# Eighteen routing pieces called four attention positions earlier in an attention-then-experts kernel

## The chip, the core and the metric

The kernel runs on one core of a Trainium2 chip. The metric is the device time of one launch in microseconds; the time before is the median of three runs. The engines are named as in the profile: PE (matmul), PEld (its weight load), DVE (vector), ACT (scalar), POOL (GpSimd) and SP, which here only issues transfers.

## What is computed

Chunked attention over 8 sequences of 576 tokens with 8 heads of 64, whose output x (4608 tokens of 512 numbers) goes through a mixture of 8 experts. Which expert a token uses depends on its own logits and, through a gate, on the token before it.

```
scores = scale * q_chunk @ k_chunk.T            # chunks of 64 tokens
attn   = softmax(scores);  x = attn @ v_chunk   # x: [B, S, 512]
logits = x @ w_gate;  gate = sigmoid(x @ w_local)
for b, s:                                       # in order along a sequence
    e = argmax(logits[b, s]) if s == 0 or gate[b, s] < 0.5 else prev_e
    h = relu(x[b, s] @ w1[e])                   # 512 -> 1024
    out[b, s] = p[e] * (h @ w2[e])              # 1024 -> 512
```

## The kernel before, in words

**Attention.** The 4608 tokens are cut into 18 attention tiles of 256 (numbers 0 to 17). A software pipeline runs iterations i = 1 to 15 (loop at L845). In each, PE does, in the order of the string `steady`: scores of tile i+1 (L214), transposes of the finished x of tile i-2 (L177, `tx`), the first half of the value products of tile i-1 (L263, `va`), transposes of q and k of tile i+2 (L177, `tq`), the router's logits of tile i-2 (L306), the second half of the values, two small logit transposes (L317, L319) and the transposes of the softmax numbers of tile i (`tp`). DVE takes the maxima (L225), subtracts them (L228), divides the value products (L275 to L277) and writes the logits to `L` (L326). The second half of the values reuses the PSUM tile `o` that DVE's first division reads, so PE waits for that division. POOL copies q and k of tile i+3 into pairs of heads (L169, token `pr`), which PE transposes in the next iteration.

**Transfers.** SP issues every load of q, k, v and weights, and the stores of finished x tiles to the DRAM buffer `x_d` (L335), in one fixed order. A load of v into one of three buffers waits until PE has done with that buffer. The finished tiles of the first iterations stand in spare weight space; tiles 6 to 8 and 14 to 17 share three buffers named `xs`, so the division of tile 17 cannot write until the store of tile 14 has read its buffer out.

**Routing of the first half.** When the logits of tokens 0 to 2303 (18 blocks of 128, attention tiles 0 to 8) are known, eighteen pieces sort them by expert: the fresh choice (s1a, s1b), the gate's scan along the sequence (s2 to s8), one-hots and counts (s9 to s11), the rank within an expert (`rank`), `after_a`, one-hot rows `rh` by rank (L452, of which twelve go to POOL and six to DVE), and two steps that turn them by 18 small matmuls (L587) into the index lists `gidx` and `sidx`. The last piece, `early_gather`, has POOL gather the first two blocks of 128 sorted tokens from `x_d` into raw1[0] and raw1[1] (L626). The pieces are called at "hooks" in the steady loop: position 4i + h is hook h of iteration i (h0 after DVE's maxima, h1 and h2 after the two router steps, h3 at the end). A list of numbers sets them.

**Around it.** Weights w1 of expert 0 land in raw1 and are split into a rounded part (ACT, L841) and a remainder (POOL, L842) at the end of iteration 13 (parts 0 and 1) and 15 (part 2). The store of x tile 8 is also called at the end of iteration 13. After iteration 15 comes the drain, a hand-written order in which the last attention tiles, the second half's routing and the first three expert blocks of 128 tokens are mixed; `x0` in it transposes gathered block 0 (L620). Then one expert block follows another (L659, L673) to the end.

Of the kernel before, what the change touches and what calls it, by code (L numbers as in the profile page):

```python
# [59 lines left out]
    "t2": "AVAA",  # L60
    "steady": "lq s*8 s h0 tx*8 s va*4 va tq*8 ra*2 h1 tq*8 pr*4 va*4 lv va ra*2 h2 tp*8 s h3 ",
    "stores": {5: (0,), 6: (1,), 7: (2,), 8: (3,), 9: (4,), 10: (5,), 11: (6,), 12: (7,), 13: (8,), 14: (9,), 15: (10, 11)},
    "hooks": [47, 47, 49, 49, 51, 51, 53, 54, 55, 55, 57, 58, 58, 59, 59, 61, 62, 62],
}


# [1076 lines left out]
```

## Time and profile before

| | us |
|---|---|
| median of 3 runs | 667.67 (667.2 to 672.87) |
| the profiled execution | 668.65 |
| its span in the profile | 666.8 |
| PE busy | 629.7 (94%) |
| DVE busy | 361.2 (54%) |
| ACT busy | 264.9 (40%) |
| POOL busy | 149.8 (22%) |

The span goes from the first to the last instruction; 1.85 us of the profiled execution lie around it. Busy shares are means over stages with different limits; in timelines a bracket gives the idle time before a row and what ended it.

### The profile page before, as it was taken

The page shows a single profiled execution, that of the slowest core. Times are in us where ns is not written, and L with a number is a line of the kernel's source. Part 1 is how long each engine was busy: PE and PEld are TensorE (multiplying, and loading weights), DVE is VectorE, ACT ScalarE, POOL GpSimd, SP SyncE. Part 2 cuts the span into 40 slices and gives each one's busy share as a digit, 9 for nine tenths or more (in the row PEclk, how much of TensorE's full clock was granted, in tenths as well). Part 3 has the DMA queues.
Part 4 walks back from the last instruction along what each step waited for, and adds up shares of the span by engine and source line. Part 5 has one row for each costly group of instructions (what it writes and reads, how often), then busy time and mean ns, then how long its engine had stood idle before and what let it go on. Part 6 is the DMA issues. An engine that isn't in the chain of part 4 may idle for free.

```text
span 666.8 us, 16364 instructions
## 1 busy us (share of the span) xinstructions
PE 629.7 (94%) x5684; PEld 501.7 (75%) x5684; DVE 361.2 (54%) x936; ACT 264.9 (40%) x439; POOL 149.8 (22%) x214
## 2 busy tenths in 40 slices
PE   3899999988999999999999999999999999999993
PEld 2778788765678877778888777788877888768882
DVE  1667768784895566662422566642566423564230
ACT  2667676755412244451221453512455222442220
POOL 3422333562040212121211212121121211112101
PEclk9999999989999999999999999999999999999998
DMA  8999999999723114644111154550248511244101
GB/s 199 261 207 271 255 257 251 275 234 322 228 80 102 62 39 163 198 170 148 50 50 34 47 179 166 172 184 33 78 146 281 182 34 35 66 160 169 48 19 38
DMA packets 85420, 98.22 MB, mean 147 GB/s; under 512 B 42388, under 2 KB 61844, under 8 KB 85268
## 3 DMA queue, kind: packets, MB, share of 16 engines
q1 hardware_dynamic: 71236, 61.01, 32.7%
q0 software_dynamic: 6640, 20.65, 9.5%
q10 hardware_dynamic: 7392, 14.68, 6.5%
q8 instruction: 77, 1.26, 0.8%
q14 instruction: 75, 0.61, 0.3%
HBM read 77.28 MB, written 20.35 MB: 146 GB/s over the span
## 4 chain that ended last, share of the span: by engine, by line
PE 44%; issue 27%; DMA 22%; DVE 4%; SPq 1%; POOLq 1%; POOL 1%; DVEq 0%
DMA out<-ysb,sidx 14%; PE y L673 12%; PE h L659 12%; PE tr L177 7%; DMA qk<-in_k 4%; PE o L263 3%; PE sc L214 2%; PE tr L753 2%; DMA x_d<-xs 1%; PE lg L306 1%; SPq L140 1%; DMA raw<-x_d,gidx 1%; PE tr L738 1%; PE y L680 1%; PE h L667 1%
## 5 line engine op out<-in xcount | busy, mean ns | idle before, releaser
L673 PE MATMUL y<-w2h,hp 128*128 128x512 f32 x560 | 185.8, 401 | 1.2 <-ACTq L1021 1.2
L659 PE MATMUL h<-w1h,xp 128*128 128x512 f32 x560 | 161.5, 398 | 0.0
L788 POOL DMA_INDIRECT out<-ysb,sidx x41 | 40.8, 995 | 371.4 <-DVE ysb L785 284.1
L673 PEld LDWEIGHTS y<-w2h,hp 128*128 128x128 f32 x560 | 105.2, 188 | 24.9 <-ACTq L978 1.4
L659 PEld LDWEIGHTS h<-w1h,xp 128*128 128x128 f32 x560 | 102.1, 188 | 20.0
L673 PE MATMUL y<-w2l,hp 128*128 128x512 f32 x280 | 110.6, 395 | 0.0
L659 PE MATMUL h<-w1l,xp 128*128 128x512 f32 x280 | 87.3, 393 | 0.5 <-DVEq L978 0.5
L726 ACT CAST hp<-tr 128x512 fp32r<-128x512 f32 x64 | 34.9, 589 | 119.9 <-PE tr L753 117.2
L785 DVE TENSOR_SCALAR ysb<-y,ppr 128x512 f32<-128x512 f32 x35 | 26.2, 750 | 87.4 <-PE y L673 72.3
L659 PEld LDWEIGHTS h<-w1l,xp 128*128 128x128 f32 x280 | 52.5, 188 | 12.4 <-DVEq L978 1.0
L673 PEld LDWEIGHTS y<-w2l,hp 128*128 128x128 f32 x280 | 52.7, 188 | 11.1 <-DVEq L978 0.2
L712 ACT ACTIVATE hsb<-h 128x1024 f32<-128x1024 f32 x35 | 35.9, 1026 | 59.4 <-PE h L659 56.5
L169 POOL COPY qk<-qk 128x512 f32<-128x512 f32 x69 | 40.4, 617 | 80.9 <-PE tr L177 53.4
L727 DVE TENSOR_TENSOR xp<-tr,xp 128x512 fp32r<-128x512 f32 x32 | 22.1, 690 | 59.8 <-ACTq L978 57.1
L177 PE MATMUL tr<-ident,qk 128*128 128x128 f32 x288 | 42.5, 293 | 12.0 <-POOL qk L169 5.5
L727 DVE TENSOR_TENSOR hp<-tr,hp 128x512 fp32r<-128x512 f32 x64 | 41.6, 685 | 15.8 <-ACT hp L726 14.1
L645 ACT ACTIVATE pex<-pex 128x8 f32<-128x8 f32 x41 | 8.6, 210 | 102.6 <-DVE pex L644 90.7
L167 ACT COPY qkT<-tr 128x512 f32<-128x512 f32 x69 | 37.6, 589 | 28.3 <-PE tr L177 21.0
L177 PEld LDWEIGHTS tr<-ident,qk 128*128 128x128 f32 x288 | 33.3, 149 | 19.5 <-POOL qk L169 9.3
L626 POOL DMA_INDIRECT xg<-x_d,gidx x39 | 41.2, 1056 | 14.1 <-issue 10.1
L753 PEld LDWEIGHTS tr<-ident,hsb 128*128 128x128 f32 x274 | 32.0, 140 | 9.0 <-ACTq L978 3.3
L753 PE MATMUL tr<-ident,hsb 128*128 128x128 f32 x274 | 37.3, 274 | 1.4 <-DVEq L978 1.4
(213 smaller groups left out, 798.8 us busy)
## 6 DMA issues: line engine op xcount, KB each, us to landing
raw<-in_moe_w SPq DMA_DIRECT2D x14, 1024.0 KB
raw<-in_moe_w ACTq DMA_DIRECT2D x14, 1024.0 KB, 7.6
raw<-in_moe_w SPq DMA_DIRECT2D x16, 512.0 KB, 4.2
qk<-in_q SPq DMA_DIRECT2D x11, 512.0 KB, 7.0
qk<-in_k SPq DMA_DIRECT2D x11, 512.0 KB, 8.3
v<-in_v SPq DMA_DIRECT2D x22, 256.0 KB, 5.5
x_d<-xs SPq DMA_DIRECT2D x7, 521.0 KB, 8.1
x_d<-x_w2h SPq DMA_DIRECT2D x6, 521.0 KB, 6.6
```

The lines of the kernel that those rows point to most:

```text
L167: eng.copy(dst, src)
L169: eng.tensor_copy(dst, src)
L177: nc.tensor.transpose(box["ps"][:, n], src_of(n), ident)
L626: nc.gpsimd.indirect_dma_start(out=dst, out_offset=None, in_=src, in_offset=bass.IndirectOffsetOnAxis(ap=gidx[t].bitcast(U32), axis=0))
L659: nc.tensor.matmul(hs[:, j], xs[a][:, c], W1[w][c][:, 512 * j:512 * j + 512], start=(c == 0 and n == 0), stop=(c == 3 and n == 2))
L673: nc.tensor.matmul(y, hx[f // 4][a][:, f % 4], W2[w][c][:, f % 2, :], start=(f == 0 and n == 0), stop=(f == 7 and n == 2))
L712: nc.scalar.activation(hsb, hs.rearrange("p j f -> p (j f)"), AF.Relu)
L726: nc.scalar.copy(p[:, 0], ps)
L727: V.tensor_tensor(p[:, 1], ps, p[:, 0].bitcast(F32), ALU.subtract)
L753: nc.tensor.transpose(ps[:, n], hsb[:, at + P * n:at + P * n + P], ident)
L785: either(kind and kind[1], lambda: V.tensor_scalar(ysb, y, pr, None, ALU.mult), lambda: y_part(ysb, y, pr))
L788: nc.gpsimd.indirect_dma_start(out=out, out_offset=bass.IndirectOffsetOnAxis(ap=sidx[t].bitcast(U32), axis=0), in_=ysb, in_offset=None, bo ...
```

## The change

One list of numbers differs. Every one of its eighteen entries is smaller by 4, so each routing piece is called exactly one iteration earlier, at the same hook in it. No instruction is added or removed. SP's order is the same row for row.

```
-    "hooks": [47, 47, 49, 49, 51, 51, 53, 54, 55, 55, 57, 58, 58, 59, 59, 61, 62, 62],
+    "hooks": [43, 43, 45, 45, 47, 47, 49, 50, 51, 51, 53, 54, 54, 55, 55, 57, 58, 58],
```

On POOL, around the end of iteration 13, before: `qk_2486` to `qk_2489` are the pair copies for attention tile 16, `qk_2665` to `qk_2668` those for tile 17, `w1l` the remainders of the weights, and the rows named DMA the gathers.

```order
L169 COPY qk_2489<-qk 128x512
L842 TENSOR_TENSOR w1l_77<-raw_0_83,w1h_73 128x512 x2
L842 TENSOR_TENSOR w1l_78<-raw_0_83,w1h_74 128x512 x2
L169 COPY qk_2665<-qk 128x512
L169 COPY qk_2666<-qk 128x512
L169 COPY qk_2667<-qk 128x512
L169 COPY qk_2668<-qk 128x512
L452 TENSOR_SCALAR rh<-iota_m,rq 128x128 x12
L626 DMA raw_0_83<-x_d,gidx_2921 128x521 x2
```

The same place on POOL in the changed kernel, where the copies for tile 17 are named `qk_2708` to `qk_2711`:

```order
L169 COPY qk_2499<-qk 128x512
L452 TENSOR_SCALAR rh<-iota_m,rq 128x128 x12
L842 TENSOR_TENSOR w1l_77<-raw_0_83,w1h_73 128x512 x2
L842 TENSOR_TENSOR w1l_78<-raw_0_83,w1h_74 128x512 x2
L169 COPY qk_2708<-qk 128x512
L169 COPY qk_2709<-qk 128x512
L169 COPY qk_2710<-qk 128x512
L169 COPY qk_2711<-qk 128x512
L626 DMA raw_0_83<-x_d,gidx_2768 128x521 x2
```

The twelve one-hot rows moved from behind four weight remainders and four pair copies to ahead of them; the two gathers still follow the copies.

On DVE, behind the rank pieces (their last rows are L834 and the six L452), a piece of the difference: which tile's maxima (L225) and subtractions (L228) stand there, those of scores called in iteration 15 (`mx_2790`) before and those of iteration 14 (`mx_2630`) now.

```order
 L834 TENSOR_SCALAR cnt<-cnt 128x1
 L452 TENSOR_SCALAR rh<-iota_m,rq 128x128 x6
-L225 TENSOR_REDUCE mx_2790<-sc 128x8
-L225 TENSOR_REDUCE mx_2792<-sc 128x8
-L228 TENSOR_TENSOR pr<-sc,mx_2790 128x512
-L228 TENSOR_TENSOR pr<-sc,mx_2792 128x512
+L225 TENSOR_REDUCE mx_2630<-sc 128x8
+L225 TENSOR_REDUCE mx_2632<-sc 128x8
+L228 TENSOR_TENSOR pr<-sc,mx_2630 128x512
+L228 TENSOR_TENSOR pr<-sc,mx_2632 128x512
```

The same batch of rank work moved ahead of the softmax of the iteration before.

## Rows read from the trace of the kernel before

**Rows 1.** The page's head and its first part: busy us, share, instructions.

```profile
span 666.8 us, 16364 instructions
PE 629.7 (94%) x5684; PEld 501.7 (75%) x5684; DVE 361.2 (54%) x936; ACT 264.9 (40%) x439; POOL 149.8 (22%) x214
DMA  8999999999723114644111154550248511244101
```

**Rows 2.** PE's waits over the whole run: us in total, times, longest.

```profile
PE o L263 <- DVE xs L277: 2.7, 2, 2.4
PE tr L620 <- DMA raw<-x_d,gidx: 2.6, 1, 2.6
```

**Rows 3.** Windows: length, busy us of PE, PEld, DVE, ACT, POOL; clock, DMA, GB/s.

```profile
86.64:94.08 7.44, 7.44 (x173) 6.16 (x172) 5.42 (x15) 5.25 (x10) 2.34 (x4) 1.00 0.94 254
...
125.33:133.35 8.02, 7.85 (x175) 6.42 (x174) 5.73 (x15) 6.37 (x12) 6.57 (x7) 1.00 1.09 263
133.35:145.35 12.00, 9.53 (x191) 7.73 (x190) 11.35 (x48) 5.51 (x10) 7.68 (x14) 0.86 0.92 232
```

**Rows 4.** Timeline of DVE in iteration 15: start, us, instruction.

```profile
133.39 0.45 DVE L427 TENSOR_TENSOR_SCAN inc<-tr,zrow 128x144 f32<-128x144 f32 x1
...
137.63 1.27 DVE L225 TENSOR_REDUCE mx<-sc 128x8 f32<-128x512 f32 x2
...
140.44 0.69 DVE L277 TENSOR_TENSOR xs<-o,rs 128x512 f32<-128x512 f32 x1
```

**Rows 5.** Timeline of PE, iteration 15 to the start of the drain.

```profile
133.35 1.16 PE L214 MATMUL sc<-qkT 64*64 64x64 f32 x64
...
136.10 1.09 PE L177 MATMUL tr<-ident,qk 128*128 128x128 f32 x8
...
141.19 0.70 PE L263 MATMUL o<-v,pT 64*64 64x65 f32 x32 [2.41 <-DVE xs L277]
...
145.35 1.16 PE L214 MATMUL sc<-qkT 64*64 64x64 f32 x64
```

**Rows 6.** Timeline of POOL, iterations 14 and 15.

```profile
126.78 4.99 POOL L842 TENSOR_TENSOR w1l<-raw,w1h 128x512 fp32r<-128x512 f32 x4 [3.44 <-ACT w1h L841]
131.69 2.30 POOL L169 COPY qk<-qk 128x512 f32<-128x512 f32 x4
136.33 7.04 POOL L452 TENSOR_SCALAR rh<-iota_m,rq 128x128 bf16<-128x128 bf16 x12 [2.34 <-DVE qsA L832]
146.18 1.18 POOL L626 DMA_INDIRECT raw<-x_d,gidx  x1 [2.81 <-issue]
```

**Rows 7.** Timeline of PE in the drain, its two longest waits there.

```profile
154.03 0.63 PE L620 MATMUL tr<-ident,raw 128*128 128x128 f32 x4 [2.65 <-DMA raw<-x_d,gidx]
...
167.80 0.35 PE L263 MATMUL o<-v,pT 64*64 64x65 f32 x8 [1.10 <-DVE xs L326]
```

**Rows 8.** Timeline of DVE in the drain, the division of tile 17.

```profile
166.96 0.69 DVE L277 TENSOR_TENSOR xs<-o,rs 128x512 f32<-128x512 f32 x1 [1.77 <-DMA x_d<-xs]
```

**Rows 9.** The chain that ended last: start, us, two transfers of it.

```profile
146.18 7.71 DMA raw<-x_d,gidx
...
158.21 8.65 DMA x_d<-xs
```

**Rows 10.** Timeline of SP, the last load of v and the store of tile 14.

```profile
141.92 1.45 SPq L153 DMA_DIRECT2D v<-in_v  x2
...
158.21 0.37 SPq L335 DMA_DIRECT2D x_d<-xs  x1
```

**Rows 11.** Windows of 2 us in the drain, columns as in rows 3.

```profile
142.00:144.00 2.00, 1.93 (x25) 1.68 (x25) 1.90 (x9) 0.00 (x0) 1.37 (x3) 0.50 0.70 250
...
152.00:154.00 2.00, 0.00 (x0) 0.00 (x1) 0.32 (x1) 0.00 (x0) 0.39 (x1) 1.00 1.03 273
...
162.00:164.00 2.00, 2.00 (x33) 1.49 (x31) 1.61 (x2) 0.00 (x0) 0.00 (x0) 1.00 1.05 392
164.00:166.00 2.00, 2.00 (x31) 1.61 (x22) 0.37 (x2) 1.17 (x2) 0.00 (x0) 1.00 0.71 171
```

## The prediction

> **What bounds the kernel now.** I read the page's first two parts first: PE is busy 94% of 666.8 us, so only time in which PE stands still is to be won, and the line of DMA digits shows the transfers near full through the first 180 us [rows 1]. Then PE's waits over the whole run: two of those in the stretch that the change touches are long, 2.4 us for a DVE division and 2.6 us for a gather [rows 2]. The windows by iteration show where the first lies: a steady iteration takes 7.44 us, the last one 12.00, with PE busy for 9.53 of it [rows 3]. The timelines of DVE, PE, POOL and SP from 125 to 168 us show the rest.
>
> In the last steady iteration, which starts at 133.35, DVE works off the rank pieces of the routing from 133.39 until the maxima get their turn at 137.63: 4.24 us in front of the softmax. The division that PE's second half of the values waits for is pushed to 140.44, and PE stands for 2.41 us until 141.19 [rows 4, 5]. That is the first wait. In the drain PE stands for 2.65 us until 154.03, because gathered block 0 is issued at 146.18 and lands 7.71 us later [rows 6, 7, 9]. At 167.80 PE waits again, for 1.10 us: the row names DVE's L326, but in front of that DVE itself idled 1.77 us for the store of an x tile, and its division, the work PE needs, ends at 167.65 [rows 7, 8]. That store is tile 14's: issued at 158.21, landed 8.65 us later [rows 9, 10].
>
> **The change, part by part.** The instructions are the same; eighteen pieces run one iteration earlier. So the sum has moved waits in it and nothing else.
>
> 1. *The wait for the division moves and stays.* The rank batch now stands ahead of the softmax of the iteration that began at 125.33 [rows 3]. I take its new start as 125.5, since two small matmuls of the routing now come ahead of it. The batch is 4.24 us long there too and finds the same work behind it, so that iteration takes about 12.0 us instead of 8.02 and ends near 137.5; the last one loses the batch. Effect: 0. Bounds: nothing saved, or the part that came from the clock. In the window from 142 to 144 the granted clock was 0.50, its lower level of 1.2 GHz, after PE's 2.41 us of standing, and the whole iteration had 0.86 [rows 3, 11]; that is up to 12.00 x 0.14 = 1.7 us. Whether the clock falls again after the moved wait is open; the 2.65 us wait at 152 to 154 left it at 1.00 [rows 7, 11]. By point 2 it makes no difference which it is.
>
> 2. *POOL gets a queue.* The twelve one-hot rows took 7.04 us and began 136.33 - 133.35 = 2.98 us after the start of their iteration [rows 5, 6]. Before, only the gathers were behind them. Now four weight remainders (4.99 us) and the four pair copies for tile 17 (2.30 us) are. Rows from 125.5 + 3.0 = 128.5 to 135.5, remainders to 140.5, copies to 142.8, instead of 131.69 to 133.99. PE asks for the first copy 136.10 - 133.35 = 2.75 us into its iteration, near 140.3, and gets it at 140.5 + 0.6 = 141.1: a new wait of 0.8 us. Had the iteration before been shorter by the clock's share, PE would only wait longer here. From there a steady iteration has 7.44 - 2.75 = 4.7 us left [rows 3, 5], so the drain starts near 145.8 instead of 145.35. Effect: +0.4 us. The remainders themselves are not needed before the drain's first expert block.
>
> 3. *The gather goes out earlier.* Its list is ready well before POOL is free, so it is issued behind the copies, near 142.9 instead of 146.18, and with the same 7.71 us lands near 150.6. PE asks for it 154.03 - 2.65 = 151.4, plus 0.4: 151.8. The 2.65 us wait goes. Effect so far: +0.4 - 2.65 = -2.2 us.
>
> 4. *What is late next.* This is the step that decides. 2.2 us earlier, PE comes to the division of tile 17 at 166.70 - 2.2 = 164.5. That division waits for the store of tile 14 to land [rows 8, 9]. Its issue follows PE, so it goes out near 156.0 instead of 158.2. But the windows show the transfer engines full all the way, 1.03 from 152 to 154 and 1.05 from 162 to 164, with the share falling to 0.71 only from 164 on, just before the store's landing at 166.86 [rows 9, 11]. A transfer that waits behind a full queue lands when the queue has been worked off, not 8.65 us after its issue. The queue holds the same loads and stores; so the landing stays at about 166.9, and PE's wait there grows from 1.1 to about 3.3 us. Bounds of the effect: +2.2 (landing fixed) or 0 (landing moves with the issue); I take +2.2, nearest to the rows on DMA share. On this the Trainium skill says, in "DMA: Bandwidth & Descriptors", section "Queues, rings and completion order", that a transfer engine consumes a ring's descriptors in ring order and takes turns between queues by packets. By that the store, on SP's queue, waits for all older loads; the share of 1.05 agrees, and the sum by the rule is the one here, 0 net, while the issue's 8.65 us taken as a latency would give -2.2.
>
> 5. *SP's queue could also come late.* The last load of v is issued at 141.92, right when PE's second half of the values, which ends at 141.19 + 0.70 = 141.89, lets the buffer go [rows 5, 10]. Without the wait that half would have started 141.19 - 2.41 - 136.10 = 2.7 us after the first transposes; now these start at 141.1, so it runs from 143.8 to 144.5, and SP's later stores and loads stand behind the load for 2.6 us more. Bounds: 0, if enough older transfers are still queued, or the whole 2.6 us on the landing of point 4. The two earlier gathers use the room in the meantime (the share was 0.70 from 142 to 144 [rows 11]) and no longer lie between the loads at 150 to 154. I take +0.2.
>
> Sum: 0 + 0.4 - 2.65 + 2.25 + 0.2 = +0.2 us. The span would be 667.0 instead of 666.8, the execution 668.85 instead of 668.65. That execution lies 0.98 above the median of the runs; against the median, 667.67 + 0.2 = 667.9. After 168 us nothing is moved.
>
> **The rivals.**
>
> *The gain comes through (faster).* The landing of tile 14's store moves with its issue, and point 4 costs nothing. For it: the share of 0.71 at 164 to 166 shows a queue that is nearly empty when the store lands, so an earlier issue could profit a little. Against it: everything before 164. Time: 667.67 + 0.4 - 2.65 = 665.4.
>
> *SP falls behind (slower).* The one mechanism is the last load of v, held back by PE's wait on POOL's late copies. If the transfer engines run dry at 144 to 146, all 2.6 us reach the landing at 166.9, and PE with it: 667.67 + 2.6 = 670.3. It decides from the point at which the queue in front of that load is shorter than 2.6 us. For it: at 142 to 144 the share is already down to 0.70. Against it: the gathers fill that gap.
>
> *The clock pays.* The wait of point 4 is then PE's longest in the drain, 3.3 us. If the clock falls behind it as it fell behind 2.41 us, that costs up to 1.7 us: 669.6. The Trainium skill, "TensorE: Matmul & The Clock Gate", section "What's actually happening", says that the default state is throttled and activity releases it, which speaks for such a loss behind any long wait. Here one wait of about 2.5 us shows it and one does not [rows 11].
>
> *Nothing moves.* If POOL's queue is longer than counted and the gather goes out no earlier than 146, the old waits stay: 667.7. Within the likeliest case's range.
>
> **How the numbers follow.** The wait moves and the time stays: 0.55, with its own range from 667.2 to 668.8. Gain comes through: 0.2. SP falls behind: 0.12. The clock pays: 0.13. The forecast is 667.9. The range of 8 in 10 reaches to the rivals on both sides, from 665.2 to 670.6. About 1% (6.7 us) is what a measurement of this kernel can tell from no change. No case gets there by itself, the two slow ones together not either; what is left is for something I have not seen: faster 0.02, same 0.95, slower 0.03.
>
> **What would show it.** Right: in the changed profile the 2.4 us wait for the division stands near 131 to 133; POOL's copies for tile 17 start near 140.5 and PE waits about a microsecond for them; the gather is issued near 143 and the 2.65 us wait on it is gone; the wait at the division of tile 17 is 3 us or more and ends within half a microsecond of 167.8. Wrong in point 4: that wait stays near 1 us and ends near 165.6. Wrong in point 2: PE does not wait for the copies, or waits more than 3 us. Wrong in point 5: the store of tile 14 lands after 168. Wrong altogether: a difference that is already there before 125 us or arises after 200.

## The result, and the profile after

The change makes the kernel a little slower: 675.16 us (672.04 to 680.43) against 671.88 (667.2 to 677.02) for the kernel before on the same chip, a ratio of 1.0057 with the 95% interval [1.0035, 1.0080]. The forecast was 667.9 against 667.67, a ratio of 1.0003, and its range ended at 670.6, a ratio of 1.0044. Against the 671.88 of this chip the loss is 3.3 us by the medians, 3.8 by the ratio.

The profiled execution of the changed kernel took 675.16 us, its median. That of the kernel before took 668.65, which lies 3.2 us below the median of its later runs, so of the 6.5 us between the two profiles (spans of 673.3 and 666.8) about half is that draw, that is, chance in which execution was profiled. Head of the page after, to be laid beside [rows 1]:

```profile
span 673.3 us, 16364 instructions
PE 632.6 (94%) x5684; PEld 503.7 (75%) x5684; DVE 367.8 (55%) x936; ACT 265.0 (39%) x439; POOL 150.7 (22%) x214
```

The same instructions, but DVE is busy for 6.6 us more. That should not happen when work is only moved. Windows over three stretches, up to the start of iteration 11, from there to the division of tile 17, and the rest (length, busy us of PE, PEld, DVE, ACT, POOL; clock, DMA, GB/s). Before:

```profile
0.00:101.50 101.50, 86.97 (x1884) 71.85 (x1884) 61.23 (x149) 60.94 (x105) 34.31 (x89) 1.00 0.99 240
101.50:168.00 66.50, 58.61 (x1205) 46.72 (x1204) 48.38 (x150) 41.27 (x72) 29.61 (x39) 0.97 1.00 275
168.00:666.80 498.80, 484.13 (x2604) 383.11 (x2597) 251.60 (x638) 162.73 (x263) 85.86 (x86) 0.99 0.33 111
```

After:

```profile
0.00:101.00 101.00, 87.29 (x1884) 72.24 (x1884) 61.41 (x149) 60.93 (x105) 34.35 (x89) 1.00 0.98 240
101.00:174.00 73.00, 61.21 (x1206) 48.47 (x1205) 54.74 (x150) 41.31 (x72) 29.44 (x39) 0.95 0.92 253
174.00:673.00 499.00, 484.12 (x2596) 382.98 (x2595) 251.66 (x638) 162.73 (x263) 86.94 (x86) 1.00 0.33 111
```

The 6.5 us arise in the middle stretch alone, and so do DVE's 6.4. The transfer engines' share fell from 1.00 to 0.92. The timeline of DVE after, at the place where the index lists are made:

```profile
138.72 0.15 DVE L590 COPY inv<-tr 128x6 f32<-128x6 f32 x1
138.91 6.49 DVE L592 SCALAR_TENSOR_TENSOR id<-inv 128x3 f32<-128x3 f32 x1
145.32 0.16 DVE L595 CAST gidx<-inv 128x3 int32<-128x3 f32 x1
...
149.47 0.69 DVE L277 TENSOR_TENSOR xs<-o,rs 128x512 f32<-128x512 f32 x1
```

An instruction on 128x3 numbers lasts 6.49 us; in the profile before it took 0.16:

```profile
144.05 0.16 DVE L592 SCALAR_TENSOR_TENSOR id<-inv 128x3 f32<-128x3 f32 x1
```

The timeline of POOL after, beside [rows 6]:

```profile
131.20 7.04 POOL L452 TENSOR_SCALAR rh<-iota_m,rq 128x128 bf16<-128x128 bf16 x12 [4.58 <-DVE qsA L832]
138.21 4.95 POOL L842 TENSOR_TENSOR w1l<-raw,w1h 128x512 fp32r<-128x512 f32 x4
143.11 2.27 POOL L169 COPY qk<-qk 128x512 f32<-128x512 f32 x4
147.37 1.18 POOL L626 DMA_INDIRECT raw<-x_d,gidx  x1 [1.99 <-issue]
```

The long instruction ends at 145.40, and POOL's four remainders and four copies end at 145.38. Before, POOL stood idle when the index lists were made (144.05 to 145.5, [rows 6]). The softmax (from 146.65) and the division of iteration 15 stand behind that instruction on DVE. PE after, beside [rows 5, 7]:

```profile
125.32 0.55 PE L177 MATMUL tr<-ident,qk 128*128 128x128 f32 x3 [1.69 <-issue]
...
143.77 1.21 PE L177 MATMUL tr<-ident,qk 128*128 128x128 f32 x8 [1.63 <-POOL qk L169]
...
150.22 1.15 PE L263 MATMUL o<-v,pT 64*64 64x65 f32 x32 [3.65 <-DVE xs L277]
...
159.56 0.60 PE L620 MATMUL tr<-ident,raw 128*128 128x128 f32 x4
...
173.53 0.35 PE L263 MATMUL o<-v,pT 64*64 64x65 f32 x8 [1.32 <-DVE xs L326]
```

PE waits 1.63 us for the pair copies and then 3.65 us for the division. The wait of 2.65 us for the gathered block at L620 is gone. At 125.32 a standstill of 1.69 us ends, for which the profile names no cause (`issue`); the kernel before did not have it at that place. The windows of iterations 13 to 15, beside [rows 3]:

```profile
118.45:129.48 11.03, 9.34 (x175) 7.65 (x174) 6.82 (x21) 4.78 (x8) 2.40 (x4) 0.85 1.09 291
129.48:139.33 9.85, 8.56 (x191) 6.63 (x191) 9.44 (x35) 6.96 (x13) 8.13 (x13) 1.00 0.92 246
139.33:153.70 14.37, 9.10 (x173) 7.49 (x173) 12.56 (x23) 5.35 (x10) 8.18 (x10) 0.88 0.56 150
```

PE began iteration 13 of the kernel before here:

```profile
116.95 1.16 PE L214 MATMUL sc<-qkT 64*64 64x64 f32 x64
```

So the changed kernel is 1.5 us late at the start of iteration 13, 4.15 at that of iteration 14 (129.48 against 125.33) and 5.98 at that of iteration 15 (139.33 against 133.35). In this pair of profiles most of the lag is there before the long instruction begins at 138.91; iteration 15 adds 2.4 us to it, and the drain gives 2.8 back by block 0. What the long instruction costs can therefore not be read from this pair; it takes a kernel that differs in nothing else (`psum_all` below).

In iteration 15 the transfers run at a share of 0.56, where they had 0.92 before. SP's waits show one reason: it held the next loads of v back until PE let a buffer go (waits in total, how many, the longest).

```profile
SPq L153 <- PE o L263: 15.1, 2, 11.6
```

So the reading is that a small DVE instruction beside POOL's queue stops DVE, DVE stops PE, and PE stops SP's queue. The experiments test the first link, and what it costs.

### The profile page after: what moved, and what is told of

It is laid out like the page before. It is cut to its first block, busy times and chain, and to the rows that moved or that the text cites. A ratio compares the mean times of both kernels' runs of the same rounds, so it can differ in the third digit from the quotient of the medians.

```text
span 673.3 us, 16364 instructions
## 1 busy us (share of the span) xinstructions
PE 632.6 (94%) x5684; PEld 503.7 (75%) x5684; DVE 367.8 (55%) x936; ACT 265.0 (39%) x439; POOL 150.7 (22%) x214
## 4 chain that ended last, share of the span: by engine, by line
PE 45%; issue 26%; DMA 20%; DVE 5%; SPq 1%; ACT 1%; POOLq 1%; POOL 0%; DVEq 0%
DMA out<-ysb,sidx 14%; PE y L673 12%; PE h L659 12%; PE tr L177 7%; DMA qk<-in_k 3%; PE o L263 3%; PE sc L214 2%; PE tr L753 2%; DMA x_d<-xs 1%; SPq L140 1%; PE lg L306 1%; PE tr L738 1%; PE y L680 1%; DVE id L592 1%; PE lg L317 1%
```

## The experiments

Ratios are to the kernel before on the same chip. In the expectations, theory P is that DVE is shut out while POOL works on SBUF. Theory C stands for chance in `again`, and for code that arrives late from `light_queue` on.

**again: the change once more.** No edit.

> The changed kernel once more, unedited. Its first profile had four things that the prediction did not: DVE's L592, 3 numbers wide, took 6.49 us beside POOL's remainders and pair copies (it took 0.16 us before); PE waited 3.65 us for the division behind it; PE stood 1.69 us in the middle of transposes for nothing that the profile names; and the clock fell twice. Theory P (DVE is shut out while POOL works on SBUF): L592 is again over 5 us and ends with POOL's last pair copy, and the division costs PE 3 us or more again. Theory C (a chance of that one execution): L592 is near 0.2 us here. Both expect the 1.69 us standstill to be gone or elsewhere, and a ratio to the kernel before of 1.003 to 1.008.

Measured: 675.05 us, ratio 1.0049 [1.0015, 1.0083]. L592 lasts 6.49 us again, from 140.33 on, beside POOL's remainders and copies, which end at 146.80. PE's standstill between the transposes returns with 2.43 us. So neither the loss nor the long instruction nor the standstill is a chance of one execution.

**psum_operand: the two-operand instructions read one operand from PSUM.** `pv` is the product in PSUM, of which `inv` is the copy in SBUF; L598 and L602 likewise. Their result `id1` is kept in PSUM, so L599 and L604 read that there.

```
-            V.scalar_tensor_tensor(id1, inv[:, 0], float(P), inv[:, 1], ALU.mult, ALU.add)
+            V.scalar_tensor_tensor(id1, pv[:, 0], float(P), inv[:, 1], ALU.mult, ALU.add)
```

> The changed kernel, but in the last routing step of the first half every DVE instruction that took two operands from SBUF takes one of them from PSUM (id1 is kept in PSUM, the others read the matmul's result there). Same work, same order, POOL untouched. Theory P with two operands (POOL shuts out only DVE instructions that read two tensors from SBUF): the step's ten instructions take about 0.2 us each, 2 us together, PE's wait for the division in the last iteration falls from 3.65 to under 1 us, and the time falls by 2.5 to 5 us against the changed kernel, to a ratio near 0.997 to 1.000. Rival, any DVE instruction that reads SBUF is shut out: the next one that reads only SBUF (the integer ones on gidx) takes 5 to 6 us instead, and the ratio stays at 1.005. Rival, the late pair copies alone make the loss: the ratio stays at 1.005 with L592 short.

Measured: 671.82 us, ratio 1.0023 [0.9989, 1.0057]. DVE at that place:

```profile
136.93 0.17 DVE L593 SCALAR_TENSOR_TENSOR tr<-tr,inv 128x3 f32<-128x3 f32 x1
137.00 6.34 DVE L596 CAST gidx<-inv 128x3 int32<-128x3 f32 x1
```

The instruction with a PSUM operand takes 0.17 us, and the next one, a cast from SBUF to SBUF with one source, is held for 6.34 instead. So it is not only a matter of two SBUF sources. On the price this run decides nothing: its interval holds both no loss and that of the change.

**one_input: POOL's four remainders of parts 0 and 1 become plain copies.** The subtraction is left out, so the first expert's numbers are not the reference's.

```
+                nc.gpsimd.tensor_copy(lo, raw) if c < 2 else
                 nc.gpsimd.tensor_tensor(lo, raw, hi.bitcast(F32), ALU.subtract)
```

> The changed kernel, but POOL's four remainders of parts 0 and 1 of w1 are plain copies of the raw weights, which read one tensor instead of two (the subtraction of the rounded part is left out). Theory P with POOL's two-operand instructions as the cause: L592 falls to about 0.2 us. Theory P with any POOL instruction that reads SBUF: L592 still lasts until POOL's last pair copy, about 4 x 0.6 + 2.3 = 4.7 us after the copies begin, less what of them had run before L592. Copies are shorter than subtractions (0.6 instead of 1.24 us), so PE's wait for the pair copies (1.63 us) goes in either case, and the time falls by 1 to 4 us against the changed kernel.

Measured: 671.98 us, ratio 1.0002 [0.9963, 1.0040]; L592 is held 3.81 us, from 140.91 until the end of POOL's copies at 144.71. A POOL run with one source per instruction holds DVE too; it is only shorter.

**splits_late: the remainders behind the pair copies, the gather at 60.**

```
-        for c in {13: (0, 1), 15: (2,)}.get(i, ()):
+        for c in {14: (0, 1), 15: (2,)}.get(i, ()):
```

> The changed kernel, but the split of parts 0 and 1 of w1 (ACT's rounding, POOL's remainder) is called at the end of iteration 14 instead of 13, and the gathers two hooks later, behind it. All work kept. POOL then has only the pair copies behind the one-hot rows. Theory P: beside the last routing step POOL runs the pair copies alone; if copies shut DVE out too, L592 takes about 2.3 us, if only the remainders do, 0.2 us; PE waits under 0.5 us for the copies; ratio 0.994 to 1.000, since the gather comes out about as late as before and its wait in the drain partly returns. Rival, the loss comes from the rank batch in front of iteration 14's softmax: the ratio stays at 1.005.

Measured: 672.74 us, ratio 1.0014 [0.9979, 1.0049]; L592 is held 1.56 us, until the four copies end. In all four runs the hold ends with POOL's uninterrupted run, whatever its length. Their times, though, can't be told from one another: a shorter hold is not shown to be a shorter kernel.

**kinds and kinds_mid: which DVE instructions are held, beside which POOL work.** Two kernels of their own. They leave the computation out. In the first each small instruction starts at the same moment as POOL's run, in the second it comes 0.7 us into it, and POOL's instructions write to different tiles.

> A kernel of its own that leaves the whole computation out and writes one tile to the output: nine kinds of small DVE instruction (128x3) are each released by a memset of POOL that is followed at once by a run of POOL work on other tiles: 4 subtractions of 128x512, 8 copies of 128x512, 8 one-hot rows of 128x128 bf16, 12 memsets of 128x512. Theory P1 (any DVE instruction with a source and a destination in SBUF and no PSUM operand is shut out until POOL's run ends): scalar_tensor_tensor, tensor_tensor, tensor_scalar, copy, cast last 4 to 5 us beside the subtractions, about 4 us beside the copies. Theory P2 (only two SBUF sources, and casts and copies): tensor_scalar, reciprocal and the reduction stay under 0.3 us. Both: sources in PSUM are not held, and nothing is held beside memsets, which read nothing; beside the bf16 one-hot rows the traces showed no held instruction, so under 0.7 us.

> The kernel of small DVE kinds again (it leaves the whole computation out), with two differences: POOL's instructions write to different tiles, so that none waits for the one before it, and DVE first reduces 128x512 (about 0.6 us, never held), so that the small instruction arrives while POOL's first or second instruction is running. POOL runs: 4 subtractions; 8 copies; 8 bf16 one-hot rows; 2 subtractions then 4 copies. Theory R (DVE must wait until POOL's queue of SBUF work has run dry): scalar_tensor_tensor, tensor_tensor, tensor_scalar, copy and cast last 3.5 to 4.5 us beside the subtractions and 3 to 4 us beside the copies. Theory I (it waits for the running instruction only): at most 1.3 and 0.6 us. Both: reciprocal, reduction and instructions with PSUM stay under 0.3 us, and nothing is held beside the bf16 rows.

Timeline of DVE in `kinds`, two rows beside POOL's memsets:

```profile
156.31 0.16 DVE L52 TENSOR_TENSOR tt<-tok 128x3 f32<-128x3 f32 x1 [6.74 <-POOL tok L65]
163.29 0.53 DVE L53 TENSOR_SCALAR ts<-tok 128x3 f32<-128x3 f32 x1 [6.82 <-POOL tok L65]
```

Timeline of DVE in `kinds_mid`: beside subtractions, three beside copies, one with an operand in PSUM, and one beside subtractions followed by copies:

```profile
3.10 0.62 DVE L53 SCALAR_TENSOR_TENSOR stt<-tok 128x3 f32<-128x3 f32 x1
...
47.49 3.75 DVE L53 SCALAR_TENSOR_TENSOR stt<-tok 128x3 f32<-128x3 f32 x1
...
52.16 0.41 DVE L54 TENSOR_TENSOR tt<-tok 128x3 f32<-128x3 f32 x1
...
70.31 0.17 DVE L58 RECIPROCAL rec<-tok 128x3 f32<-128x3 f32 x1
...
83.76 0.15 DVE L61 SCALAR_TENSOR_TENSOR stp<-tok,ps 128x3 f32<-128x3 f32 x1
...
149.08 3.98 DVE L57 CAST casti<-tok 128x3 int32<-128x3 f32 x1
```

Held beside fp32 subtractions and copies in `kinds_mid`: scalar_tensor_tensor, tensor_tensor, tensor_scalar, copy and cast, where all operands lie in SBUF. In `kinds` the same five were not held beside the subtractions, with whose run they start (0.16 to 0.17), and beside the copies for one copy only (0.61 to 0.62), where theory P1 had 4 to 5 us and about 4. Never held in either (0.15 to 0.18): reciprocal, reduction, and whatever has a PSUM operand. Beside the bf16 one-hot rows they took at most 0.32 us. For how long varies: in `kinds_mid` ten of the fifteen instructions of these five kinds beside fp32 work came through at the next change of POOL's instruction (0.41 to 0.62 us), two at a later change (2.87, 3.43), three only at the end of the run (3.75 to 3.98). Neither theory R nor I holds alone: at each change of POOL's instruction DVE may get in or not. In the seven profiles of attention kernels with a hold it never got in before the end of the run.

The Trainium skill, "SBUF — State Buffer", sections "SBUF: two separate sides" and "Who interferes with whom", says that DVE and GpSimd share a pair of ports as an exclusive lock, taken by copies, casts and tensor_scalar in their two-port forms, and by instructions with two SBUF inputs against a GpSimd instruction that reads SBUF, and that reductions never contend. The kinds of the two runs agree as far as the page names them, also that memsets held the tensor_scalar (0.53) and not the tensor_tensor (0.16). It says further that the loser waits for the instruction that came first. Here it waited for up to eight; the measurement stands.

**held_before: the hold put into the kernel before.** POOL's halves of the first two splits move behind the one-hot rows, which is at the end of iteration 14; ACT's halves stay.

```
-            run(w1_split(c))
+            run(w1_split(c)[0::1 + (c < 2)])
...
-    hq = sg + [lambda: run(sg_rank()), after_a, lambda: run(sg_onehots())] + sl + [early_gather]
+    hq = sg + [lambda: run(sg_rank()), after_a, lambda: (run(sg_onehots()), [run(w1_split(c)[1::2]) for c in (0, 1)])] + sl + [early_gather]
```

> The kernel before with POOL's four remainders w1l of parts 0 and 1 called behind the one-hot rows of iteration 15 instead of at the end of iteration 13 (ACT's halves stay). POOL then subtracts from about 143.4 to 148.4, just when DVE makes the index lists (144.05). Theory P: L592 or a neighbour of it, 0.16 us before, lasts 3.5 to 5 us and ends with POOL's last remainder; the gather is issued near 149.5 to 151 instead of 146.18, and the kernel is slower than before by 2 to 4 us (ratio 1.003 to 1.006). Theory N (long rows on DVE beside POOL are a peculiarity of the moved order): L592 stays at 0.16 us, the gather is near 148.5, behind the remainders in POOL's order, and the kernel is slower by at most 2.4 us (ratio up to 1.0035).

Measured: 679.78 us, ratio 1.0110 [1.0069, 1.0151]. DVE:

```profile
144.30 4.28 DVE L592 SCALAR_TENSOR_TENSOR id<-inv 128x3 f32<-128x3 f32 x1
```

POOL:

```profile
143.59 4.96 POOL L842 TENSOR_TENSOR w1l<-raw,w1h 128x512 fp32r<-128x512 f32 x4
150.55 1.18 POOL L626 DMA_INDIRECT raw<-x_d,gidx  x1 [2.00 <-issue]
```

PE:

```profile
158.81 1.09 PE L620 MATMUL tr<-ident,raw 128*128 128x128 f32 x4 [4.96 <-DMA raw<-x_d,gidx]
```

The hold appears in the old order as soon as POOL is at work there, and ends with POOL's last remainder at 148.55. The loss, some 7 us, is larger than the 2 to 4 us expected, and not all of it is the hold: the gather is 4.4 us later than in [rows 6], of which POOL's new order alone was expected to make 2.3 (148.5). The profile is of one of the two shortest of its six runs. In it PE waits 4.96 us for the gather instead of 2.65, and behind that wait the granted clock was 0.50, its lower level of 1.2 GHz, which the kernel before did not show there.

**psum_all: the change without the hold.** Every one of the small instructions of the first list gets an operand in PSUM (`pv`, `gp`, `od`, `pad`), by keeping scratch numbers beside the product.

```
+                gp, od, pad = pinv[:, 260:260 + Q].bitcast(I32), pinv[:, 280:280 + Q], pinv[:, 300:300 + Q]
...
-            V.tensor_copy(gi, inv[:, 0])
+            V.tensor_copy(gp, pv[:, 0])
...
-            V.scalar_tensor_tensor(odd, odd, float(HT), id1, ALU.mult, ALU.add)
+            V.scalar_tensor_tensor(od, od, float(HT), id1, ALU.mult, ALU.add)
```

> The change, with every small DVE instruction of the index lists (L592 to L604 there) given one operand in PSUM, by keeping the scratch numbers beside the product in the same PSUM bank; same instructions, same order, same results. Theory P (DVE is shut out only where all its operands are in SBUF, while POOL has SBUF work): none of the ten lasts over 0.5 us, PE's wait for xs L277 after the pair transposes of iteration 15 (3.65) falls under 1 us, and the time falls by 2 to 4 us against the change: ratio to before 0.998 to 1.002. Theory Q (the hold is a detour that costs nothing; the loss comes from the early pieces, POOL's later pair copies and the late block of code): the long instruction is gone, but the ratio stays at 1.003 to 1.007.

Measured: 670.54 us, ratio 0.9997 [0.9963, 1.0031]. DVE:

```profile
136.76 0.16 DVE L599 SCALAR_TENSOR_TENSOR id<-tr,inv 128x3 f32<-128x3 f32 x1
136.83 0.16 DVE L600 CAST tr<-tr 128x3 int32<-128x3 f32 x1
```

POOL:

```profile
136.05 4.96 POOL L847 TENSOR_TENSOR w1l<-raw,w1h 128x512 fp32r<-128x512 f32 x4
140.95 2.28 POOL L169 COPY qk<-qk 128x512 f32<-128x512 f32 x4
143.41 1.18 POOL L631 DMA_INDIRECT raw<-x_d,gidx  x1 [0.17 <-POOL qk L169]
```

PE, and the chain that ended last:

```profile
133.90 0.70 PE L263 MATMUL o<-v,pT 64*64 64x65 f32 x32 [1.25 <-DVE x_w2l L277]
...
168.19 0.35 PE L263 MATMUL o<-v,pT 64*64 64x65 f32 x8 [2.32 <-DVE xs L326]
```

```profile
157.39 9.87 DMA x_d<-xs
```

With POOL's order unchanged and only the operands' place changed, the hold is gone and with it the loss: 1.0057 - 0.9997 = 0.0060, some 4 us of 671, though the two intervals leave 1 to 7. This is the run that decides for P. In its profile iteration 15 takes 8.70 us (137.74 to 146.44) where the change takes 14.37, at about the same granted clock (0.87 and 0.88). A standstill of 1.69 us is in this profile too, so it is not what `psum_all` wins.

**s2_late, pair_first, choice_early: the change in parts.** `s2_late` keeps the last two pieces at 62. `pair_first` keeps fourteen pieces early and restores POOL's order. `choice_early` moves the first twelve alone.

```
-    "hooks": [43, 43, 45, 45, 47, 47, 49, 50, 51, 51, 53, 54, 54, 55, 55, 57, 58, 58],
+    "hooks": [43, 43, 45, 45, 47, 47, 49, 50, 51, 51, 53, 54, 54, 55, 55, 57, 62, 62],
+    "hooks": [43, 43, 45, 45, 47, 47, 49, 50, 51, 51, 53, 54, 54, 55, 58, 59, 62, 62],
+    "hooks": [43, 43, 45, 45, 47, 47, 49, 50, 51, 51, 53, 54, 58, 59, 59, 61, 62, 62],
```

> The change with its last two pieces (the turn of the one-hots into index lists, and the gather) left at position 62, the other sixteen at 43 to 57. POOL's copies and remainders then end before the index lists are made. Theory P (the loss is DVE shut out by POOL's run of SBUF work): L592 lasts under 0.3 us instead of 6.49; PE's wait for xs L277 after the pair transposes of iteration 15 (3.65) falls under 1 us; the ratio to before is 0.998 to 1.003, with the gather near 148 to 150 and some of the wait of 2 to 2.65 for it back. Theory Q (the loss comes from the early fourteen pieces themselves: the pieces' work on DVE and the standstill of 1.3 to 2.4 us in PE's transposes after L422): L592 may be short, but the ratio stays at 1.004 to 1.007.

> The first fourteen pieces as in the change (positions 43 to 55, the rank at 54), but the one-hot rows at 58, behind the pair copies of iteration 14, then 59, 62, 62: POOL's order is that of the kernel before row for row. No hold, no wait for POOL's pair copies. Theory Q1 (loss by POOL's order and the hold): the division wait of 2.4 us is gone, PE's standstill at the code block (1.3 to 2.4) stays, the wait for gathered x is 1 to 2.7: ratio 0.997 to 1.001. Theory Q2 (loss by the pieces' earlier work on DVE and PE itself): ratio 1.003 to 1.007 with POOL's order restored.

> Only the first twelve pieces (fresh choice, scan, one-hots, counts) at 43 to 54; rank and all behind it as before. The division wait of 2.4 us behind the rank batch is back at the place of before. Theory Q1: ratio 1.000 to 1.003 (the late block of code, 1.3 to 2.4 us, is the only cost, partly covered since transfers bound this stretch). Theory Q2: ratio 1.003 to 1.007. Beside pair_first it gives the worth of the early rank: 0 by the prediction on record (the wait moves and stays), 2.4 us if it goes.

Measured: 677.37 us, 1.0071 [1.0036, 1.0106]; 675.10 us, 1.0065 [1.0033, 1.0096]; 671.83 us, 1.0008 [0.9975, 1.0040]. In none is an index instruction held, so two of them are slower for another reason, and my expectation for both was wrong. Windows of `pair_first`, from iteration 11 to the start of iteration 14, and 12 us around its transposes of gathered block 0:

```profile
100.67:132.31 31.64, 26.41 (x525) 21.17 (x525) 20.91 (x63) 16.47 (x29) 7.16 (x12) 0.92 1.08 258
156.00:168.00 12.00, 9.82 (x98) 7.69 (x88) 4.02 (x12) 5.42 (x10) 3.90 (x4) 0.57 0.94 329
```

The same two stretches of the kernel before:

```profile
101.53:125.33 23.80, 23.16 (x523) 19.10 (x522) 19.43 (x58) 16.85 (x31) 7.22 (x12) 1.00 1.00 269
151.00:163.00 12.00, 9.35 (x131) 6.77 (x122) 5.92 (x17) 6.41 (x11) 3.63 (x4) 1.00 1.04 347
```

`pair_first` takes 7.8 us longer for its early iterations, 4.2 us of it in two standstills that no semaphore explains (2.37 and 1.87), and loses later to the clock: after a wait of 2.18 us for gathered block 0 the clock is at 0.57. In `s2_late` the same wait is 4.17 us, and the clock is at 0.73 from 156 to 168. The early pieces do not bring the early loss every time: `psum_all`, with the same fourteen pieces early, took 25.90 us for the three iterations, `s2_late` 26.44 and the change 28.45. That the two kernels, whose gather goes out late behind an early rank, are 4 to 5 us slower than the one before is measured; how much of it is the clock and how much the standstills stays open.

**light_queue, psum_light: is it the load ahead of the code?** The standstill of 1.69 us in the changed kernel, and most of those like it in the other kernels, sit at the same instruction of PE. In the changed kernel a packet of code moves a little before it ends at 125.32. The DMA queues from 123.0 to 124.2, among 264 packets of data:

```profile
q1 hardware_dynamic: 264, 0.44, 100.0%
q8 instruction: 1, 0.02, 4.9%
```

The Trainium skill, "Runtime: NRT & Kernel Launch", section "Instruction fetch mechanics", says that an engine's code is fetched in blocks of 16 KiB over a DMA queue while it runs, at a cost that is mostly hidden. The packet's size agrees; whether the standstill is part of that cost the traces do not show. The test leaves out the 1 MB load of w1 that SP issues ahead of it, in the change and in `psum_all`, and has POOL fill the place with a constant.

```
-        for c in {11: (0, 1), 13: (2,), 14: (3,)}.get(i, ()):
+        for c in {5: (0, 1)}.get(i, ()):
+            nc.gpsimd.memset(raw1[c], 0.01)
+        for c in {13: (2,), 14: (3,)}.get(i, ()):
             load_w1(0, c)
```

> The change with the 1 MB load of the weights w1, parts 0 and 1, left out: POOL fills raw1[0] and raw1[1] with a constant in iteration 5 instead (so the first expert's numbers are not the reference's). Theory C (PE's standstill in the transposes after L422, 1.3 to 2.4 us in every kernel with the moved hooks, is PE's next block of code arriving late behind the data in full DMA queues): the standstill falls under 0.5 us, and the time is shorter than the change by 1.5 to 4 us. Theory S (it belongs to the place in the program, and not to the load of the queues): 1.3 to 2.4 us stay. In both DVE's L592 is held for 4 to 6.5 us. If the queues bound the front, its end comes about 3 us earlier (1 MB at some 300 GB/s).

> psum_all (no hold) without the 1 MB load of w1, parts 0 and 1; POOL fills them with a constant in iteration 5 instead, so the first expert's numbers are not the reference's. Theory C (the block of code behind that load takes the gain): the standstill at the transposes after L422 falls from 1.69 under 0.4 us, and the ratio to before falls to 0.992 to 0.996. Theory T (transfers and the wait at tile 17's division take it): the standstill goes, the wait at tile 17's division grows beyond 2.32 or the front ends 1 to 2 us earlier only, and the ratio is 0.996 to 1.000.

Measured: 673.22 us, ratio 1.0037 [1.0007, 1.0067], and 668.62, ratio 0.9975 [0.9949, 1.0002]. PE at that place in `light_queue`, then in `psum_light`:

```profile
121.81 1.04 PE L177 MATMUL tr<-ident,qk 128*128 128x128 f32 x8
```

```profile
124.94 0.55 PE L177 MATMUL tr<-ident,qk 128*128 128x128 f32 x3 [1.88 <-issue]
```

Gone in one, still there in the other. So that load alone does not make the standstill, and theory C falls in this form. In `psum_light` the wait at tile 17's division is 2.19 us, where theory T had it grow beyond 2.32 or the front end only 1 to 2 us earlier; its ratio is in theory T's range.

The two kernels also repeat the comparison of the change with `psum_all`. DVE in `light_queue`:

```profile
135.61 6.51 DVE L592 SCALAR_TENSOR_TENSOR id<-inv 128x3 f32<-128x3 f32 x1
```

In `psum_light` the same step (L599 there, from 138.24) takes 0.16 us. The ratios lie 0.0062 apart, as the first pair's lie 0.0060, and here too the intervals leave 1 to 7 us.

**psum_w1_12, psum_w1_10, psum_w1_10b, before_w1_10: the load of w1 elsewhere.** The load is issued an iteration later (the split at the end of 14, the gather at 60) or earlier; the last kernel is the one before with the earlier load alone.

```
-        for c in {11: (0, 1), 13: (2,), 14: (3,)}.get(i, ()):
+        for c in {10: (0, 1), 13: (2,), 14: (3,)}.get(i, ()):
```

> psum_all with that load issued at the end of iteration 12, the split of these parts at the end of iteration 14 and the gather called at 60 behind it. Theory C: the block of code at the transposes after L422 comes in time (standstill under 0.4 us) and the ratio is 0.993 to 0.998, since the gather is later by the remainders' place in POOL's order but still ahead of x0. Theory T: ratio 0.998 to 1.003.

> psum_all with the load of w1, parts 0 and 1, issued at the end of iteration 10 instead of 11. Nothing is left out. Theory C: the load then stands ahead of another block of code; the standstill moves or shrinks; ratio 0.994 to 1.001 depending on where PE meets the next late block. Theory T: ratio within 0.002 of psum_all's 0.9997.

> psum_w1_10 once more, unedited. If 0.9945 was no chance of the draw: ratio 0.992 to 0.998, below before_w1_10 if the gain needs the early pieces. Otherwise 0.998 to 1.002, as psum_all (0.9997).

> The kernel before with the load of w1, parts 0 and 1, issued at the end of iteration 10 instead of 11; nothing else. If the load alone brings the gain: ratio 0.993 to 0.997. If the gain needs the early pieces without the hold: ratio 0.998 to 1.003.

Measured: 671.02 us, 1.0018 [0.9987, 1.0048]; 667.13 us, 0.9945 [0.9915, 0.9975]; 668.43 us, 0.9953 [0.9916, 0.9990]; 671.10 us, 0.9986 [0.9950, 1.0022]. PE in `psum_w1_10b` at tile 17's division:

```profile
165.92 0.35 PE L263 MATMUL o<-v,pT 64*64 64x65 f32 x8 [2.92 <-DVE xs L326]
```

In both, `psum_w1_10` is ahead of the kernel before, by some 3 to 4 us: the early pieces without the hold and with an earlier load beat both kernels. Whether the load alone does a part of it can't be told, since the interval of `before_w1_10` overlaps. The standstill at the code was 2.15 us in one and 0.23 in the other, so it does not decide this gain either.

## Why the prediction was wrong

**The step that failed** is in point 3: "Its list is ready well before POOL is free". The list could not be made until POOL was free. Point 2 had put the remainders and copies right where DVE makes the index lists, and priced what PE waits for behind them (POOL's results), not what DVE can't do beside them. The missing term is the hold: 6.49 - 0.16 = 6.33 us on DVE, of which PE felt 3.65 at the division, and some 4 us of the whole by `psum_all`. No rival had it. The sum also says that it "has moved waits in it and nothing else", and so has no term for the standstill of 1.69 us (2.43 in `again`). The prediction's own sign of being wrong altogether, a difference before 125 us, did appear: 1.5 us at the start of iteration 13. The cause of the standstill stays open; `psum_all` has it too and is as fast as the kernel before.

**Point 1, the division wait moves and stays: right in length without the hold, wrong in the wait.** Iteration 14 was to run from 125.5 to 137.5. In `psum_all` it ran from 126.03 to 137.74, but PE waited only 1.25 us for the division (133.90), where the kernel before had 2.41 an iteration later. In the change it began at 129.48, took 9.85 us, and PE did not wait for the division in it.

**Point 2, POOL gets a queue: right.** Rows, remainders, copies in that order, 7.04, 4.95 and 2.27 us; without the hold the copies start at 140.95 (forecast 140.5). PE waited 1.63 us for them in the change (forecast 0.8; more than 3 was to refute it). In `psum_all` it hardly waited (less than 0.2 us), since it came later itself: the granted clock was 0.57 from 136 to 140.

**Point 3, the gather: right once the hold is gone.** Without the hold the list is ready at 138.0, well before POOL is free at 143.2. `psum_all` issues the gather at 143.41 (forecast 142.9), and the wait for block 0 is gone. In the change it went out at 147.37, 1.99 us after POOL's last copy. Even so the wait for block 0 was gone, because the front was later still.

**Point 4, the landing stays and the next wait grows: right without the hold.** In `psum_all` tile 14's store lands at 157.39 + 9.87 = 167.26 (forecast 166.9), the wait is 2.32 us (forecast 3.3) and ends at 168.19 (forecast within half a microsecond of 167.8). All five profiles without the hold and with an early gather show this wait, 2.19 to 3.06 us long. In the change the landing, 172.59, came 8.87 us after its issue, much as before (8.65), and the wait was 1.32. The low share of 0.56 in iteration 15 does not explain that: `psum_all` ran low at that place too, and its landing took 9.87.

```profile
136.00:146.00 10.00, 9.73 (x178) 8.04 (x179) 6.33 (x22) 5.36 (x9) 9.37 (x11) 0.83 0.69 174
```

Why the landing moved with its issue in the one and not in the other stays open.

**Point 5, SP's last load of v: right in kind, wrong in size.** It was to cost 0.2 us through a load held back by PE for 2.6 us; the change holds these loads back by up to 11.6 us. Without the hold the last load of v went out 4.3 us later than before (146.23 against 141.92), and the gathers did not fill the room: the share fell to 0.20 and 0.35 between 142 and 146. Tile 14's store nevertheless landed only 0.4 us later than before.

**The sum.** Without the hold the steps' sum, +0.2 us or 1.0003, stands beside a measured 0.9997 [0.9963, 1.0031]. That it fits is in part luck: PE came to tile 17's division 0.8 us earlier than before (165.87 against 166.70) and not 2.2, with the standstill, which no term has, on the way; the wait for the store, which was to be 3.3 us, took up the difference. With the hold the kernel is 0.6% slower, within the 1% that had the chance of 0.95, but outside the range of 8 in 10.

## What to carry to other kernels

When work is moved on POOL, read also what DVE runs at that time: a small instruction with all its operands in SBUF can wait for POOL's whole run, and everything behind it on DVE waits too. A duration that grew in a profile where work was only moved is the sign. An operand left in PSUM ended the hold here and won the time back; a place where POOL is idle ended it too, but the kernel that had that and the early rank (`s2_late`) stayed slow. And where a gain ends in a wait for a store, try the transfers as well: with the load of w1 an iteration earlier the early pieces gained 3 to 4 us, though why is not shown.

## What was not expected of the hardware

In the attention kernels an instruction of 0.16 us waited 1.56 to 6.51 us, always to the end of POOL's run of up to eight instructions, while in `kinds_mid` ten of fifteen such instructions came through at POOL's next change. What decides that was not found. PE also stood still for up to 2.4 us at places where no semaphore held it, in most kernels with the pieces moved, by no more than 0.4 us in the profile before, but by 1.19 in `before_w1_10`, whose pieces are not moved. In the one trace looked at, a packet of code moved just before. Leaving out the load ahead of it removed this once and not the second time.
